# Single PSUM banks in a ring of eight, and score tiles in pairs, in a clustered-attention kernel

## The chip, the cores and the metric

The kernel runs on one core of one Trainium2 chip. The time is the device time of one execution in microseconds, and the number that counts is the median of the runs: 749.23 us over 3 runs (748.53 to 749.55).

## The reference

Three blocks run one after the other. In the first, queries and keys of 16 heads (batch 2, 8 heads, 768 positions, 64 channels) each choose the nearest of 16 centroids, and a query attends only to keys of its own cluster:

```python
q_assign = argmax(q_n . c_n);  k_assign = argmax(k_n . c_n)
mask = q_assign[:, :, :, None] == k_assign[:, :, None, :]
scores = where(mask, scale * q @ k^T, -1e9)
attn = softmax(scores);  x = attn @ v            # (2, 768, 512)

theta = x @ w_theta
y = w_tok_r @ (x * cos(theta)) + w_tok_i @ (x * sin(theta))
u = x + y;  x = u + max(u @ w_ch, 0)

u = x + (x^T @ U @ V)^T
out = u + max(u @ w_ch1, 0) @ w_ch2
```

## The kernel before, in words

Everything is unrolled by hand, and each engine runs its instructions in the order in which the Python code issues them. `manual_schedule` keeps that order. A tile is allocated when the code asks for it, from the tiles of its pool whose last use has been issued; the instruction that first writes it waits until that last use is over.

*Memory.* 59 SBUF slots of 128x768 fp32 serve all large tiles (`slot`, L52). PSUM has eight banks. Six form three tiles of two banks (`ps2`, L55); two more form one tile for the value product and, later, for every second theta and feed-forward tile (`pv2`, L58).

*Attention* goes over 8 clusters of work `g`: two heads of one batch entry. (The word cluster below means such a unit.) The mask is folded into the score product as one-hot rows. Precision comes from splitting fp32 numbers into a high and a low part, so scores take two passes. For each cluster:
- `assign_items` (L101) finds the nearest centroid: one group of matmuls (`sims`), then six VectorE operations. `split_hi`, `split_lo`, `pack` (L173 to L214) split queries and keys on ScalarE and GpSimd and copy the parts into packed tiles by DMA from SP, and `mask_rows` or `mask_direct` write the one-hot rows.
- `max_tile` (L225) multiplies a tile of 128 queries with all keys (two matmuls of 384 columns, into two banks) and VectorE takes the maximum of 768 columns (L233). `max_rows` (L242) turns the maxima into two rows of the packed tile, so that they are subtracted by the score product.
- `scores` (L259) makes one tile of 128 keys by 768 queries with four matmuls of 384 columns, and ScalarE takes the exponential of all 768 (L267).
- `pv` (L270) multiplies by the values; `sum_keys` (L284) sums the exponentials; `row_sums`, `spread`, `norm_x` divide.

In `attention` (L656) the loop over `g` has six steps `p`. A step issues two score tiles of cluster `g` and two maximum tiles of cluster `g+1` in turn (`ORDER`, L659), then two calls of `pv`, then background work for about 1.7 us of VectorE (`fill`, L636): items of a queue, or else conversions of float64 weights (`Convert`, L320: ScalarE L340 and L357, VectorE L344, L348, L352, GpSimd L361). From `g == 2` on, all twelve token-weight tiles are queued for conversion.

*Prologue* (L732): it loads constants, then queries and keys of clusters 0 and 1, the values of cluster 0, and queries and keys of clusters 2 and 3, nine loads of 384 KB in all; prepares the centroids; and carries cluster 0 through assignment, maxima and the first head's scores. `heat` issues matmuls that only keep TensorE running.

*Mixer* (L825): theta and token mixing over 24 steps, channel mixing (`chmix`), the low-rank block (`low1`, `low2`) and the feed-forward block (`ff1`, `ff2`), whose sums go to the output from `ff_sum` (L620).

Of the kernel before, what the change touches and what calls it, by code (L numbers as in the profile page):

```python
# [10 lines left out]
F32 = mybir.dt.float32  # L11
# [11 lines left out]
P = 128  # L23
# [17 lines left out]
def tile_cluster_block(ctx: ExitStack, tc: tile.TileContext, qk, v, cent, wth, wr, wi, wch,  # L41
# [7 lines left out]
    pp = ctx.enter_context(tc.tile_pool(name="pp", bufs=3, space=PSUM))  # L49
    pv_p = ctx.enter_context(tc.tile_pool(name="pvp", bufs=1, space=PSUM))  # L50
# [4 lines left out]
    def ps2(name, shape=None):  # L55
        return pp.tile(shape or [P, 2, 512], F32, tag="ps", name=name)

    def pv2(name):  # L58
        return pv_p.tile([P, 2, 512], F32, tag="pv", name=name)
# [41 lines left out]
    def assign_items(g):  # L101
        st = {}

        def sims():
            ps = ps2("sims")
            for i, hf, o in BLOCKS:
                nc.tensor.matmul(out=ps[o:o + 32, 0, :HALF], lhsT=cblk[:, g % NP, :], rhs=raw[g, i][:, cols(hf)],
                                 start=True, stop=True)
            st["s"] = slot("s_t")[:, :HALF]
            nc.vector.transpose(st["s"], ps[:, 0, :HALF])  # L110
# [42 lines left out]
    def mask_direct(g, h, eng):  # L153
        x = XROW[h]
        r = slice(x, x + 16)
        for i in range(2):
            ps = ps2("oht")
            for hf in range(2):
                o = 32 * (2 * i + hf) + 16 * h
                nc.tensor.matmul(out=ps[r, hf, :HALF], lhsT=identb[:, o:o + 16], rhs=onehots[g],  # L160
                                 start=True, stop=True)
            src, dst = ps[r, :, :HALF], h2((qp, kp)[i][g % SETS, h, 0][r])
            if i == 0:
                nc.scalar.activation(out=dst, in_=src, func=AF.Copy)
            elif eng is nc.scalar:
                nc.scalar.activation(out=dst, in_=src, func=AF.Identity, scale=BIG, bias=kmul[r, 2:3])
            else:
                eng.tensor_scalar(dst, src, BIG, BIG, op0=ALU.mult, op1=ALU.subtract)
# [33 lines left out]
    def pack(g, main=(0, 1)):  # L202
        s = g % SETS
        qh, ql, kh, kl = hl[g, 0, 0], hl[g, 0, 1], hl[g, 1, 0], hl[g, 1, 1]
        for h in range(2):
# [10 lines left out]
    def pack_direct(g, h):  # L216
        d, s = slice(64 * h, 64 * h + 64), g % SETS
        for t, src in ((kp[s, h, 0], raw[g, 1]), (qp[s, h, 0], raw[g, 0]), (qp[s, h, 1], raw[g, 0])):
            nc.scalar.activation(out=t[d], in_=src[d], func=AF.Copy)
        nc.gpsimd.tensor_tensor(kp[s, h, 1][d], raw[g, 1][d], f32(kp[s, h, 0][d]), op=ALU.subtract)  # L220


    mx_t = {}

    def max_tile(g, h, qt):  # L225
        s = g % SETS
        if qt == 0:
            mx_t[g, h] = small.tile([P, NT], F32, tag="mx", name="mx")
        ps = ps2("smax")
        for hf in range(2):  # L230
# [734 lines left out]
```

## Time and profile before

| what | value |
|---|---|
| median of 3 runs | 749.23 us |
| the profiled execution | 750.61 us, its span 748.8 us |
| TensorE busy (matmul) | 711.7 us, 95% |
| VectorE | 436.9 us, 58% |
| ScalarE | 294.4 us, 39% |
| GpSimd | 196.8 us, 26% |
| DMA | 64.03 MB, mean 86 GB/s |
| mean granted clock of TensorE | 0.986 |
| loads of queries and keys | 384 KB each, 16 of them |

The span is the time from the first to the last instruction. Busy times of a TensorE row add matmuls that overlap in its pipeline, so a busy share near 100% does not mean that no matmul came late; its weight loads (PEld) are separate instructions, and where one of them waits, the reason is written behind the row. The clock is a share of full speed.

### The profile page before, as it was taken

To read this page: it belongs to the slowest core of one execution; us is meant where nothing else is said; L and a number is where in the kernel's file an instruction comes from. 1 tells how busy PE (TensorE), PEld (TensorE's weight loads), DVE (VectorE), ACT (ScalarE), POOL (GpSimd) and SP (SyncE) were. 2 spreads that over 40 slices of the span, in tenths; PEclk is the share of its full clock that TensorE was granted. 3 is DMA by queue.
4 is the path that set the end of the run, shared out by engine and by line. 5 is a ranking of instruction groups with operands and counts; after the bars stand their busy time and mean duration, and the time that the engine had idled before them with its cause. 6 is when DMAs were issued, how large, how long until landed. Compare 5 with 4: busy or idle time off the path is not lost.

```text
span 748.8 us, 10420 instructions
## 1 busy us (share of the span) xinstructions
PE 711.7 (95%) x4111; PEld 557.9 (75%) x4111; DVE 436.9 (58%) x658; ACT 294.4 (39%) x485; POOL 196.8 (26%) x191
## 2 busy tenths in 40 slices
PE   6799999999899998999999799999999999999997
PEld 2555555555555558999999799888889888888885
DVE  6775877768778538545759796543543533532222
ACT  4454555545556554454653823322222222211000
POOL 8512032132433316111327450132112112100000
PEclk8799999999999999999999999999999999999999
DMA  8776385563622213000311221012212211000112
GB/s 242 172 184 214 84 215 168 127 177 99 162 71 84 85 55 115 1 1 1 113 43 54 85 84 43 1 43 85 84 43 85 85 47 67 29 1 0 57 34 79
DMA packets 21504, 64.03 MB, mean 86 GB/s; under 512 B 4272, under 2 KB 6192, under 8 KB 21456
## 3 DMA queue, kind: packets, MB, share of 16 engines
q1 hardware_dynamic: 21456, 63.37, 29.5%
q8 instruction: 32, 0.52, 0.3%
q14 instruction: 16, 0.13, 0.1%
HBM read 40.94 MB, written 3.15 MB: 59 GB/s over the span
## 4 chain that ended last, share of the span: by engine, by line
PE 83%; DVE 7%; ACT 4%; DMA 2%; issue 2%; POOL 2%; SPq 0%; DVEq 0%; POOLq 0%; ACTq 0%
PE acc L610 18%; PE g L589 17%; PE y L477 10%; PE pv L274 9%; PE st L264 8%; PE smax L231 5%; PE h L493 5%; PE l L291 4%; PE th L435 3%; DVE mx L233 2%; PE h L544 1%; DVE tht L443 1%; DMA qp<-lo 1%; DVE cv L348 1%; ACT p L267 1%
## 5 line engine op out<-in xcount | busy, mean ns | idle before, releaser
L361 POOL TENSOR_TENSOR wl<-cv,wh 128x768 fp32r<-128x768 f32 (+1 forms) x40 | 78.3, 1958 | 256.6 <-ACT wh L357 228.3
L596 DVE SCALAR_TENSOR_TENSOR gl<-g,gh 128x512 fp32r<-128x512 f32 x48 | 33.2, 692 | 156.6 <-ACT gh L594 156.6
L267 ACT ACTIVATE p<-st 128x768 f32<-128x768 f32 x96 | 76.9, 811 | 89.8 <-PE st L264 87.2
L233 DVE TENSOR_REDUCE mx<-smax 128x1 f32<-128x768 f32 x96 | 90.3, 953 | 35.4 <-PE smax L231 35.0
L594 ACT ACTIVATE gh<-g 128x512 fp32r<-128x512 f32 x48 | 28.7, 598 | 204.2 <-PE g L589 204.2
L477 PE MATMUL y<-wh,z 128*128 128x384 f32 x384 | 89.4, 345 | 8.0 <-ACT z L455 6.8
L264 PE MATMUL st<-qp,kp 128*128 128x384 f32 x384 | 88.8, 356 | 3.9 <-ACT p L267 1.7
L589 PE MATMUL g<-ul,wh 128*128 128x512 f32 (+1 forms) x256 | 86.4, 337 | 0.0
L589 PE MATMUL g<-uh,wh 128*128 128x512 f32 (+1 forms) x256 | 86.1, 336 | 0.0
L589 PE MATMUL g<-uh,wl 128*128 128x512 f32 (+1 forms) x256 | 86.0, 336 | 0.0
L264 PEld LDWEIGHTS st<-qp,kp 128*128 128x128 f32 x384 | 66.6, 192 | 25.1 <-issue 10.2
L610 PE MATMUL acc<-gh,wh 128*128 128x512 f32 x192 | 76.0, 396 | 0.6 <-DVE xT L566 0.6
L610 PE MATMUL acc<-gl,wh 128*128 128x512 f32 x192 | 75.7, 394 | 0.0
L610 PE MATMUL acc<-gh,wl 128*128 128x512 f32 x192 | 75.7, 394 | 0.0
L477 PEld LDWEIGHTS y<-wh,z 128*128 128x128 f32 x384 | 67.5, 190 | 9.3 <-ACT z L455 7.7
L274 PE MATMUL pv<-p,v 128*64 128x384 f32 x384 | 72.4, 501 | 0.0
L231 PE MATMUL smax<-kp,qp 128*128 128x384 f32 x192 | 55.7, 375 | 6.5 <-DVE mx L233 2.8
L589 PEld LDWEIGHTS g<-uh,wh 128*128 128x128 f32 x256 | 48.5, 189 | 6.2
L589 PEld LDWEIGHTS g<-ul,wh 128*128 128x128 f32 x256 | 48.4, 189 | 5.9
L589 PEld LDWEIGHTS g<-uh,wl 128*128 128x128 f32 x256 | 48.6, 190 | 5.2
L274 PEld LDWEIGHTS pv<-p,v 128*64 128x64 f32 x384 | 23.5, 136 | 34.8 <-issue 34.8
L477 PE MATMUL y<-wl,z 128*128 128x384 f32 x192 | 49.4, 339 | 0.0
(127 smaller groups left out, 1183.6 us busy)
## 6 DMA issues: line engine op xcount, KB each, us to landing
st<-in_w_dram SPq DMA_DIRECT2D x20, 768.0 KB, 4.2
raw<-in_qk_dram SPq DMA_DIRECT2D x16, 384.0 KB, 5.7
qp<-hi SPq DMA_DIRECT2D x30, 192.0 KB, 2.8
st<-in_wr_dram SPq DMA_DIRECT2D x6, 768.0 KB, 4.2
st<-in_wi_dram SPq DMA_DIRECT2D x6, 768.0 KB, 4.3
v<-in_v_dram SPq DMA_DIRECT2D x8, 384.0 KB, 4.8
kp<-hi SPq DMA_DIRECT2D x32, 96.0 KB, 2.8
qp<-lo SPq DMA_DIRECT2D x32, 96.0 KB, 2.6
```

The lines of the kernel that those rows point to most:

```text
L231: nc.tensor.matmul(out=ps[:, hf, :HALF], lhsT=qp[s, h, 0][:, qt * P:(qt + 1) * P], rhs=kp[s, h, 0][:, hf * HALF:(hf + 1) * HALF], start=Tr ...
L233: nc.vector.tensor_reduce(mx_t[g, h][:, qt:qt + 1], ps[:, :, :HALF], axis=AX.XY, op=ALU.max)
L264: nc.tensor.matmul(out=ps[:, hf, :HALF], lhsT=kp[s, h, w][:, kt * P:(kt + 1) * P], rhs=qp[s, h, w][:, hf * HALF:(hf + 1) * HALF], start=(w ...
L267: nc.scalar.activation(out=h2(t), in_=ps[:, :, :HALF], func=AF.Exp, scale=float(D) ** -0.5)
L274: nc.tensor.matmul(out=pvt[g][64 * h:64 * h + 64, hf, :HALF], lhsT=v_t[g][:, kt, 64 * h:64 * h + 64], rhs=pt[g, h, kt][:, hf * HALF:(hf + ...
L291: nc.tensor.matmul(out=ps[o:o + 32, 0, :HALF], lhsT=ones, rhs=pt[g, h, kt][:, cols(hf)], start=(kt == 3 * a), stop=(kt == 3 * a + 2))
L361: nc.gpsimd.tensor_tensor(t[:, :c.w], c.t, f32(c.hi[:, :c.w]), op=ALU.subtract)
L477: nc.tensor.matmul(out=yps[u, j][:, hf, :HALF], lhsT=lhs, rhs=w[st][e][:, hf * HALF:(hf + 1) * HALF], start=(st == 0 and n == 0), stop=(st ...
L493: nc.tensor.matmul(out=ps[:, hf, :HALF], lhsT=wv[a], rhs=xs[b, t][c][:, hf * HALF:(hf + 1) * HALF], start=(n == 0), stop=(n == 11))
L589: nc.tensor.matmul(out=ps[:, o:o + w], lhsT=wv[a], rhs=us[b, t][e][:, s0:s0 + w], start=(n == 0), stop=(n == 11))
L596: nc.vector.scalar_tensor_tensor(gl, ps, 0.0, f32(gh), op0=ALU.max, op1=ALU.subtract)
L610: nc.tensor.matmul(out=aps[c, e // 2][:, e % 2], lhsT=wv[a], rhs=g[x], start=(first and i == 0), stop=(last and i == 2))
```

## The change

Every PSUM tile becomes one bank of a ring of eight (`bank`); what needs two takes two tiles (`banks`), and its reader becomes two instructions, one per bank. Score tiles and maximum tiles are made in pairs of tiles, 1536 columns in three banks of 512: the first tile's columns 0 to 511; its last 256 beside the next tile's first 256; and the rest. ScalarE's exponentials go by the pieces (512, 256, 256, 512 columns); VectorE takes maxima of each bank, and a join takes the larger of each two.

The order of attention is by pairs too, so the value products of a cluster begin later and the last of them come in step 3 of the next; normalisation moves from step 3 to step 5. Six of the twelve token-weight tiles are queued only in the last cluster, where `fill` gets twice the budget. In the prologue, loads of clusters 2 and 3 and of the values come later, the second low split and the direct low part (`pack_direct_lo`, split off `pack_direct`, L216) come after the masks on GpSimd, the packs of cluster 0 are issued head by head, and the second cluster's assignment runs while cluster 0's maxima are turned into rows.

```diff
-    pp = ctx.enter_context(tc.tile_pool(name="pp", bufs=3, space=PSUM))
-    pv_p = ctx.enter_context(tc.tile_pool(name="pvp", bufs=1, space=PSUM))
+    pp = ctx.enter_context(tc.tile_pool(name="pp", bufs=8, space=PSUM))
+    def bank(name):
+        return pp.tile([P, 512], F32, tag="ps", name=name)
+    def banks(name):
+        return [bank(name), bank(name)]
...
+    THIRDS = [[(0, 0, 512)], [(0, 512, 256), (1, 0, 256)], [(1, 256, 512)]]
+    def max_pair(g, h, a):
+        s = g % SETS
+        if a == 0:
+            mx_t[g, h] = small.tile([P, 2 * NT], F32, tag="mx12", name="mx12")
+        o = 2 * a
+        for part in THIRDS:
+            ps, c = bank("smax"), 0
+            for j, k0, w in part:
+                nc.tensor.matmul(out=ps[:, c:c + w], lhsT=qp[s, h, 0][:, (a + j) * P:(a + j + 1) * P],
+                                 rhs=kp[s, h, 0][:, k0:k0 + w], start=True, stop=True)
+                c += w
+            n = len(part)
+            nc.vector.tensor_reduce(mx_t[g, h][:, o:o + n], ps.rearrange("p (n w) -> p n w", n=n), axis=AX.X, op=ALU.max)
+            o += n
...
+    def scores_pair(g, h, a):
+        s = g % SETS
+        for kt in (a, a + 1):
+            pt[g, h, kt] = slot(f"p{h}")
+        for part in THIRDS:
+            ps, c = bank("st"), 0
+            for j, q0, n in part:
+                for w in range(2):
+                    nc.tensor.matmul(out=ps[:, c:c + n], lhsT=kp[s, h, w][:, (a + j) * P:(a + j + 1) * P],
+                                     rhs=qp[s, h, w][:, q0:q0 + n], start=(w == 0), stop=(w == 1))
+                c += n
+            c = 0
+            for j, q0, n in part:
+                nc.scalar.activation(out=pt[g, h, a + j][:, q0:q0 + n], in_=ps[:, c:c + n], func=AF.Exp,
+                                     scale=float(D) ** -0.5)
+                c += n
...
     def ff2(c, f):
...
+            if last:
                 ff_sum(c, e, end)
...
-        ORDER = [(0, 0), (0, 1), (0, 2), (0, 3), (0, 4), (1, 0), (0, 5), (1, 1), (1, 2), (1, 3), (1, 4), (1, 5)]
+        ORDER = [(0, 0), (0, 2), (0, 4), (1, 0), (1, 2), (1, 4)]
...
+                conv_load.extend(tok[:6])
+                late = tok[6:]
+            if g == 7:
+                conv_load.extend(late)
...
+                if order[p]:
+                    h, a = order[p]
+                    scores_pair(g, h, a)
+                    if h:
+                        pvq.extend((g, kt, hf) for kt in (a, a + 1) for hf in range(2))
+                if nxt:
+                    max_pair(g + 1, p // 3, 2 * p % 6)
+                    if p % 3 == 2:
+                        max_join(g + 1, p // 3)
...
-                fill(1.7)
+                fill(1.7 if nxt else 3.4)
...
+        its, its1 = assign_items(0), assign_items(1)
         for i in range(2):
             split_hi(0, i)
-            split_lo(0, i, nc.gpsimd)
+        split_lo(0, 0, nc.gpsimd)
         run(its[:1])
         pack_direct(0, 0)
+        pack(0, main=(), heads=(0,))
+        load_v(0)
+        for i in range(2):
+            load_raw(2, i)
+
         init_packs(1, nc.gpsimd)
         heat(14)
         run(its[1:])
+        run(its1[:1])
         mask_direct(0, 0, nc.vector)
+        split_lo(0, 1, nc.gpsimd)
+        pack_direct_lo(0, 0)
+        pack(0, heads=(1,))
         for i in range(2):
             split_hi(1, i)
+        for a in (0, 2, 4):
+            max_pair(0, 0, a)
+        max_join(0, 0, act=True)
+        max_rows(0, 0)
+
+        run(its1[1:])
+        mask_direct(0, 1, nc.scalar)
+        init_packs(2, nc.gpsimd)
+        for i in range(2):
             split_lo(1, i, nc.gpsimd)
         pack(1)
+        for g in range(3, 4):
+            for i in range(2):
+                load_raw(g, i)
         bg.extend(split_items(2, nc.gpsimd))
+        for a in (0, 2, 4):
+            scores_pair(0, 0, a)
+            max_pair(0, 1, a)
+            heat(2)
+            if a == 2:
+                mask_direct(1, 0, nc.scalar)
                 while bg:
                     fill(.5)
+        max_join(0, 1)
         max_rows(0, 1)
         mask_direct(1, 1, nc.scalar)
```

## Rows read from the trace of the kernel before

**Rows 1.** The page, busy time, share and instructions of each engine.
```profile
PE 711.7 (95%) x4111; PEld 557.9 (75%) x4111; DVE 436.9 (58%) x658; ACT 294.4 (39%) x485; POOL 196.8 (26%) x191
```

**Rows 2.** Stretches: length, busy us and count by engine, clock, DMA share, GB/s.
```profile
0.00:41.60 41.60, 29.67 (x123) 16.07 (x124) 27.11 (x51) 20.28 (x28) 29.50 (x35) 0.84 0.81 207
...
62.80:245.80 183.00, 173.63 (x1106) 102.11 (x1104) 137.59 (x196) 100.54 (x129) 53.91 (x71) 0.99 0.52 140
245.80:274.50 28.70, 28.70 (x200) 15.03 (x198) 12.12 (x16) 16.70 (x22) 8.62 (x11) 1.00 0.26 83
274.50:291.00 16.50, 13.32 (x94) 12.41 (x90) 13.47 (x22) 9.03 (x21) 7.37 (x12) 1.00 0.33 102
```

**Rows 3.** Waits of weight loads in clusters 1 to 6: us, times, longest.
```profile
PEld smax L231 <- ACT p L267: 8.2, 27, 2.3
...
PEld smax L231 <- DVE mx L233: 4.1, 6, 0.7
```

**Rows 4.** Timeline of one attention step, TensorE: start us, us, instruction [idle before].
```profile
107.49 0.96 PE L264 MATMUL st<-qp,kp 128*128 128x384 f32 x4
...
109.42 0.30 PEld L231 LDWEIGHTS smax<-kp,qp 128*128 128x128 f32 x2 [0.24 <-ACT p L267]
...
109.97 1.51 PE L274 MATMUL pv<-p,v 128*64 128x384 f32 x8
...
111.41 0.31 PEld L247 LDWEIGHTS <-m 128*2 128x2 bf16 x6 [0.60 <-DVE mx L233]
```

**Rows 5.** The page, costliest groups: busy us, mean ns | idle before.
```profile
L596 DVE SCALAR_TENSOR_TENSOR gl<-g,gh 128x512 fp32r<-128x512 f32 x48 | 33.2, 692 | 156.6 <-ACT gh L594 156.6
...
L233 DVE TENSOR_REDUCE mx<-smax 128x1 f32<-128x768 f32 x96 | 90.3, 953 | 35.4 <-PE smax L231 35.0
L594 ACT ACTIVATE gh<-g 128x512 fp32r<-128x512 f32 x48 | 28.7, 598 | 204.2 <-PE g L589 204.2
```

**Rows 6.** Groups by line and shape, 45 to 270 us, ScalarE's exponentials.
```profile
L267 ACT ACTIVATE p<-st 128x768 f32<-128x768 f32 x89 | 71.3, 811 | 85.4 <-PE st L264 82.9 <-DMA qp<-hi 1.1 <-DMA raw<-in_qk_dram 0.3
```

**Rows 7.** The chain that ended last: start us, us, what.
```profile
8.48 9.51 DMA qp<-lo
22.21 3.56 DVE mx L233 x4
...
88.59 2.14 PE l L291 x24
...
295.39 4.17 PE y L477 x24
...
487.55 2.76 PE g L589 x12
...
493.11 2.87 PE g L589 x24
```

**Rows 8.** Timeline of the prologue, 0 to 45 us.
```profile
6.54 3.58 POOL L180 TENSOR_TENSOR lo<-raw,hi 128x768 fp32r<-128x768 f32 x2
...
8.24 4.06 DVE L118 TENSOR_TENSOR eqw<-s_t,mxc 128x384 bf16<-128x384 f32 x1
...
10.09 1.79 POOL L220 TENSOR_TENSOR kp<-raw,kp 64x768 fp32r<-64x768 f32 x1
...
15.79 0.96 DVE L168 TENSOR_SCALAR kp<-oht 16x768 fp32r<-16x768 f32 x1 [1.30 <-PE oht L160]
...
18.13 1.62 PE L231 MATMUL smax<-kp,qp 128*128 128x384 f32 x4 [0.64 <-DMA qp<-lo]
...
27.73 0.80 ACT L249 ACTIVATE qp<-mrow 2x768 fp32r<-2x768 f32 x1 [4.09 <-PE mrow L247]
```

**Rows 9.** Waits of matmuls over the whole span: us, times, longest.
```profile
PE h L493 <- DVE xT L497: 1.1, 2, 0.8
...
PE acc L610 <- DVE xT L566: 0.6, 1, 0.6
```

**Rows 10.** Timeline of the end: VectorE's last two adds.
```profile
744.29 1.40 DVE L625 TENSOR_TENSOR xT<-acc,xT 128x512 f32<-128x512 f32 x2 [0.35 <-PE acc L610]
```

More of the change, by code (lines that the diff above doesn't have):

```diff
@@ L244, in max_rows @@
         m2 = mx_t.pop((g, h))
-        ps = ps2("mrow")
-        for qt in range(NT):
-            nc.tensor.matmul(out=ps[x:x + 2, qt // 3, (qt % 3) * P:(qt % 3 + 1) * P], lhsT=m2[:, qt, :],
-                             rhs=identb, start=True, stop=True)
-        nc.scalar.activation(out=h2(qp[s, h, 1][x:x + 2]), in_=ps[x:x + 2, :, :HALF], func=AF.Copy)
+        for hf in range(2):
+            ps = bank("mrow")
+            for j in range(3):
+                nc.tensor.matmul(out=ps[x:x + 2, j * P:(j + 1) * P], lhsT=m2[:, 3 * hf + j, :], rhs=identb,
+                                 start=True, stop=True)
+            nc.scalar.activation(out=qp[s, h, 1][x:x + 2, cols(hf)], in_=ps[x:x + 2, :HALF], func=AF.Copy)
     pt, v_t, pvt, xT = {}, {}, {}, {}
@@ L482, in ymix @@
                 x = xT[2 * u + j]
-                nc.vector.tensor_tensor(h2(x), yps[u, j][:, :, :HALF], h2(x), op=ALU.add)
+                for hf in range(2):
+                    nc.vector.tensor_tensor(x[:, cols(hf)], yps[u, j][hf][:, :HALF], x[:, cols(hf)], op=ALU.add)
     def chmix(b, e):
-        ps = ps2("h")
+        ps = banks("h")
         n = 0
@@ L496, in chmix @@
         x = xT[b * NP + e]
[L497 removed]
+        for hf in range(2):
+            nc.vector.scalar_tensor_tensor(x[:, cols(hf)], ps[hf][:, :HALF], 0.0, x[:, cols(hf)], op0=ALU.max, op1=ALU.add)
     xt4 = {}
@@ L601, in ff2 @@
         if first:
-            for j in range(2):
-                aps[c, j] = ps2("acc")
+            for e in range(4):
+                aps[c, e] = bank("acc")
         g = gt.pop((c, f))
         end = last and f == NF - 1
-        order = (0, 2, 1, 3) if end and c == 2 else (0, 1, 2, 3)
-        for e in order:
+        for e in range(4):
             wv = wcol(w2_t, f * DM + e * P, P)
             for i, (a, x) in enumerate(PASSES):
-                nc.tensor.matmul(out=aps[c, e // 2][:, e % 2], lhsT=wv[a], rhs=g[x],
+                nc.tensor.matmul(out=aps[c, e], lhsT=wv[a], rhs=g[x],
                                  start=(first and i == 0), stop=(last and i == 2))
-            if end and c == 2 and e:
-                ff_sum(c, {2: 0, 1: 2, 3: 1}[e], end)
-            elif last and e % 2 and not (end and c == 2):
-                ff_sum(c, e - 1, end)
+            if last:
                 ff_sum(c, e, end)
-        if end and c == 2:
-            ff_sum(c, 3, end)
     def ff_sum(c, e, end):
@@ L734, in prologue @@
         nc.vector.memset(hot[:, :512], 0.0)
-        hp = pv2("hot")
+        hp = bank("hot")
         def heat(n):
             for _ in range(n):
-                nc.tensor.matmul(out=hp[:, 0], lhsT=hot[:, :P], rhs=hot[:, :512], start=True, stop=True)
+                nc.tensor.matmul(out=hp, lhsT=hot[:, :P], rhs=hot[:, :512], start=True, stop=True)
         nc.sync.dma_start(out=cst_sb, in_=cst)
```

165 lines of the change are left out of this document (57 added, 108 removed).

## The prediction

> **What bounds the kernel now.** TensorE is busy 711.7 of 748.8 us [rows 1], so I first read the table of stretches, which says where it is not, and then what it waits for there. Four stretches matter [rows 2]: the prologue (to 41.6, TensorE busy 29.67, granted clock 0.84), clusters 1 to 6 of attention (183.0 us, 173.63 busy), cluster 7 (28.7, no gap) and the start of the mixer (16.5, 13.32 busy). In the rest of the mixer the chain of waits is matmul behind matmul, so little can come from there.
>
> "Busy" hides stalls, since matmuls overlap, so for the clusters I read the weight loads, which stop at once when a bank is missing: those of the maxima waited 8.2 us for the exponentials of the tile before and 4.1 us for VectorE's maxima [rows 3]. That is a ring of three two-bank tiles at work: the second maxima of a step take the pair that the step's first exponential still reads. The timeline of one step shows the size [rows 4]: it runs from 107.49 to 111.41, 3.92 us, of which 0.24 are this wait; after it the first value product starts 0.55 us behind the last maxima's first weight load, though their two matmuls are worth 0.35.
>
> **The change part by part.** Prices first. ScalarE takes 0.598 us for 512 columns [rows 5] and 0.811 for 768 [rows 6]: 0.83 ns a column and 0.17 fixed, so I estimate 0.49 for 384 and 0.385 for 256. VectorE takes 0.953 for 768 and 0.692 for 512 [rows 5], about 0.17 fixed too. Matmuls cost 4.17/24 = 0.174 us at 384 columns, 2.76/12 = 0.230 at 512, 2.87/24 = 0.120 at 256 [rows 7].
>
> *Score and maximum pairs.* The eight score matmuls of a step become four of 512 and four of 256: 1.40 for 1.39 us; the maxima's four cost 0.70 both before and after. So the new widths cost TensorE nothing. A step is then 1.40 + 0.70, 0.2 for the last matmul's run into the value products, and 1.44 for these (109.97 to 111.41): 3.74 us. A cluster adds two key sums of 2.14 [rows 7] and, estimated from their columns, 1.4 for the rows of maxima and the assignment matmuls: 28.1 against 183.0/6 = 30.5. Six clusters could give 14 us; the two waits of [rows 3] alone are 12.3. With eight banks, two held by the value product, a bank comes back after six others, one whole step later. Against it: ScalarE gets four exponentials for two, 1.97 us for 1.62 a pair, and VectorE three maxima for two, 2.08 for 1.91, with two short joins a cluster. VectorE goes from 137.59/6 = 22.9 us a cluster to about 24.4, ScalarE from 16.8 to about 19.4; both stay under 28.1 [rows 2], and that slack is the cover. If it goes, nothing is gained here. The range is 3 to 14; I take 10.5, nearest the waits named, with some left because VectorE would be 87% busy.
>
> *Halved copies* (value output, maxima rows, sums in the mixer): 0.17 us more each on ScalarE or VectorE, hidden by TensorE's work. The deferred value products and the later normalisation add no work.
>
> *Weights held back to cluster 7.* Six of the twelve token-weight tiles now come there, with twice the filling. VectorE has room: 12.12 busy of 28.7 [rows 2]; so has GpSimd. ScalarE does not: 16.7 us now, plus the splits and up to six conversions, makes about 26, and an exponential queued behind a conversion holds the value products that need it. I take 1 us slower, between 0 and 3. The loads are issued from SP, whose queue holds no other load by then, and need a staging buffer free, not ScalarE. In return the mixer starts without conversions between the short VectorE operations of theta: of its 3.2 us of idle TensorE [rows 2] I take 2 back, between 0 and 3.2.
>
> *Prologue.* VectorE's comparison in the first assignment took 4.06 us [rows 8], because it ended only 0.42 after GpSimd's third subtraction (10.09 + 1.79 = 11.88). The change leaves one 1.79 us subtraction in front (6.54 to 8.33), so the comparison ends near 8.75, 3.55 earlier. The mask was written 4.45 us after it (16.75 against 12.30); with the second cluster's transpose put ahead, 13.8. The maxima were then held until 18.13 by a pack copy issued at 8.48 that took 9.51 us to land [rows 7, 8]; of the nine bulk loads of 384 KB ahead of it the change leaves four, so I let it land before 13.8. Nine maxima of 0.69 take 6.2, the join and its rows 2.6 (before: 25.77 to 28.53): 22.9 against 28.5. Then ScalarE sets the pace: two masks of four copies at 0.49, twelve exponentials of three pairs (5.9), two splits of 0.8: 11.4, and I add 0.7 for matmuls between them at the mean clock of 0.84 [rows 2]. Attention starts at 35 against 41.6. The second cluster's assignment, 3.5 us of VectorE, lies under masks and scores. GpSimd's list (one subtraction, eight memsets, two subtractions, eight memsets, two subtractions) ends near 28, and SP issues the sixteen copies of cluster 1 behind it, the first landing near 30: in time. Loads of clusters 2 and 3 come later on SP, cluster 3's behind all of these, but are used only in attention. The gain is 6.5, between 4 (comparison alone) and 9 (TensorE at full clock throughout, and no pause between ScalarE's pieces).
>
> *Mixer and tail.* The waits of channel-mix matmuls (1.1) and of the first accumulator (0.6) for VectorE [rows 9] go with eight banks. At the end two adds stood behind the last matmul (1.40 for two) [rows 10]; now one does: 0.7. Together 2.3, between 1.4 and 2.9.
>
> The sum is -10.5 + 1 - 2 - 6.5 - 2.3 = -20.3 us. The profiled execution took 750.61 (span 748.8), 1.4 above the median of 749.23, so it would become 730.3 and the median 728.9; I say 729.
>
> **The rivals.** *The fixed costs reach the path.* VectorE and ScalarE run in order, and TensorE may follow them after all: clusters then give nothing and the splits are paid. For it: VectorE was already 75% busy with waits of its own. Against: its waits for key sums shrink, and a bank is now due a step later. Without the 10.5 the time is 739.4, and to 741 with some of the fixed cost. The Trainium skill (VectorE: DVE Perf Modes, section on the TRN2 errata) says that each instruction of VectorE or ScalarE pays a fixed latency again, and advises tiles of 512 elements or more; by it the 256- and 384-wide pieces are a mistake, and 96 more exponentials by the 0.17 above would put 16 us onto the path, for 745 at worst. The rows agree on the fixed cost but show ScalarE at 100.54 of 183.0 us. Chance 0.17.
>
> *The prologue's gain is hidden.* The scores of cluster 0 or the packs of cluster 1 arrive late, since GpSimd's memsets now stand before the second low split: 749.2 - 13.8 = 735.4. The landing of small copies under load (9.51 us) speaks for it, GpSimd's list above against it. Chance 0.11.
>
> *Slower: SBUF slots.* Value products lag by two calls more and both probability tiles of a pair are taken at once, from the same 59 slots. A slot freed less than a step ago makes ScalarE's first exponential of a pair wait, behind it all other ScalarE work, and then the banks. In the trace an exponential waited once, 1.1 us, for a copy still reading its slot [rows 6]. At 1.1 us for each of 36 pairs it costs 39.6: 768. It decides from 20.3/36 = 0.56 us a pair. Against: it happened once in 89, and weight tiles and splits that held slots move to cluster 7. Chance 0.06.
>
> *The ring is none:* were the bank freed last handed out first, each third would wait for its reader, and a step would take about double. The rows speak against it: the second scores of a step start right behind the first maxima. Chance 0.01.
>
> **How the numbers follow.** The forecast has 0.65, with 723 to 735 as its own range. The range reaches to the fixed-cost case and down to the sum of the better ends: 721 to 741. A measurement of this kernel tells about 0.2%, 1.5 us, from no change. Faster 0.92, same 0.02, slower 0.06.
>
> **What would show it.** Right: weight loads of the maxima no longer wait for exponentials or maxima; clusters 1 to 6 take 28.5 to 29 us each; first attention maxima near 35 us, first maxima near 14; six weight conversions in cluster 7; one add after the last matmul. Wrong: VectorE without idle time in the clusters, ScalarE waiting for slots or for copies, or TensorE idle in cluster 7 behind exponentials.

## The result, and the profile after

The changed kernel takes 736.27 us (median of three runs, 735.71 to 737.27) against 749.39 for the kernel before in the same comparison: 13.1 us less, a ratio of 0.983 (95% interval 0.981 to 0.985). One more run of it was disturbed and took 1751.66 us; it is left out here, as are two such runs of r1_halves below, and with it the median is 736.77, the 736.8 that the expectations below name. The profiled execution took 736.27 us, its span is 734.5, that is 14.3 less than the profiled span of before.

First the table of stretches again, cut where the stages now begin (length, busy us and count of TensorE, its weight loads, VectorE, ScalarE, GpSimd, then clock, DMA share, GB/s):

```profile
0.00:40.86 40.86, 28.96 (x123) 15.65 (x123) 26.88 (x59) 22.35 (x43) 29.81 (x35) 0.85 0.78 199
40.86:60.36 19.50, 19.50 (x120) 10.86 (x119) 16.01 (x32) 7.50 (x18) 0.00 (x0) 0.97 0.69 178
60.36:232.36 172.00, 167.11 (x1107) 95.56 (x1105) 136.83 (x241) 100.07 (x215) 51.97 (x69) 0.99 0.56 150
232.36:267.64 35.28, 31.46 (x208) 14.46 (x206) 25.89 (x25) 23.25 (x45) 18.66 (x15) 1.00 0.35 112
```

Against [rows 2] the prologue hardly moved (40.86 for 41.60), clusters 1 to 6 lost 11.0 us (172.0 for 183.0), cluster 7 gained 6.6 (35.28 for 28.70), and what follows, the mixer to the end, went from 474.3 to 466.9. Cluster 0 lost 1.7, of which 1.44 are two calls of the value product that the change moves to the end, into cluster 7. The time lies inside the range, 7.3 above the forecast, and two of the terms are far off.

**Where the gain is.** The waits of the weight loads in clusters 1 to 6 (total, times, longest), to be set beside [rows 3]:

```profile
PEld smax L237 <- DVE mx L241: 2.2, 2, 1.2
...
PEld l L318 <- ACT p L292: 2.0, 1, 2.0
```

The maxima no longer wait for an exponential at all (8.2 us before), and for VectorE in two places only. The timeline shows what a step is now, on TensorE, VectorE and ScalarE, answering to [rows 4]:

```profile
96.12 1.68 PE L287 MATMUL st<-qp,kp 128*128 128x512 f32 x8
97.64 0.85 PE L237 MATMUL smax<-kp,qp 128*128 128x512 f32 x4
98.42 1.51 PE L300 MATMUL pv<-p,v 128*64 128x384 f32 x8
99.86 1.69 PE L287 MATMUL st<-qp,kp 128*128 128x512 f32 x8
...
98.06 1.89 DVE L241 TENSOR_REDUCE mx<-smax 128x1 f32<-128x512 f32 x3 [0.79 <-PE smax L237]
...
100.64 1.64 ACT L292 ACTIVATE p<-st 128x512 f32<-128x512 f32 x4 [2.10 <-PE st L287]
```

From 96.12 to 99.86 it is 3.74 us, the figure of the forecast. The last two lines show why the thinner pieces cost nothing: four exponentials in a row take 1.64 us, not the 1.97 of the working, and three maxima 1.89 instead of 2.08.

The gain is not even. Clusters 1 to 6 took 29.3, 29.5, 30.3, 29.5, 33.6 and 30.8 us before and take 25.1, 29.4, 28.1, 28.5, 29.9 and 31.1 after: clusters 1 and 5 alone give 7.9 of the 11.0. Cluster 5 of before holds a stretch at the lower clock behind a wait of 2.3 us for exponentials (the longest of [rows 3]):

```profile
181.47:215.05 33.58, 30.83 (x190) 17.96 (x188) 24.04 (x36) 17.80 (x23) 11.09 (x13) 0.95 0.42 100
```

After has such a stretch too, in cluster 6 (granted clock 0.95, last section), so the two nearly cancel in the sum. What still keeps cluster 5 of after over 28.1 is a slot: ScalarE's exponentials stand for 2.66 us, though their scores are there, until VectorE's comparison (L118) has read the slot that they write; TensorE's key sum stands behind them:

```profile
179.66 0.87 ACT L292 ACTIVATE p<-st 128x512 f32<-128x512 f32 x2 [2.66 <-DVE eqw L118]
180.31 2.14 PE L318 MATMUL l<-p,ones 128*32 128x384 f32 x24 [1.71 <-ACT p L292]
```

In the built program the first of these exponential tiles has the slot in which the comparison's input lay. In cluster 2 the key sum waits 1.25 us for VectorE's maxima.

**Where it was lost: cluster 7.** The chain of waits holds two entries that it did not have (start, us, what), two loads of weights that are still to be converted:

```profile
242.19 4.22 DMA st<-in_wr_dram
...
257.15 4.17 DMA st<-in_wi_dram
```

The timeline of cluster 7 shows who stands behind them:

```profile
241.22 0.89 DVE L379 SCALAR_TENSOR_TENSOR cv<-st,cv 128x768 int32<-128x768 int32 x1
...
246.49 0.91 ACT L367 ACTIVATE cv<-st 128x768 f32<-128x768 f32 x1 [6.46 <-DMA st<-in_wr_dram]
247.29 1.61 ACT L292 ACTIVATE p<-st 128x512 f32<-128x512 f32 x4
...
247.93 1.76 PE L287 MATMUL st<-qp,kp 128*128 128x512 f32 x8 [0.81 <-ACT p L292]
251.69 1.51 PE L300 MATMUL pv<-p,v 128*64 128x384 f32 x8 [2.00 <-ACT p L292]
...
261.40 0.91 ACT L367 ACTIVATE cv<-st 128x768 f32<-128x768 f32 x1 [3.39 <-DMA st<-in_wi_dram]
```

VectorE's low bits (L379) free a staging buffer at 242.1, the load issues at 242.19 and lands 4.2 us later. Meanwhile ScalarE, which works in order, is already at that tile's first operation, the magnitude (L367), and stands idle for 6.46 us; the exponentials stand behind it, TensorE behind them. Without any wait cluster 7 would take the 28.7 us of before and the 1.44 of the moved value products, 30.1: some 5.1 us are lost here.

**Where it was won and lost again: the prologue.** Timeline of all engines, to be read with [rows 8]:

```profile
8.42 0.56 DVE L118 TENSOR_TENSOR eqw<-s_t,mxc 128x384 bf16<-128x384 f32 x1
...
13.27 2.35 PE L237 MATMUL smax<-kp,qp 128*128 128x512 f32 x12 [1.24 <-ACT qp L163]
...
20.53 0.86 ACT L268 ACTIVATE qp<-mrow 2x384 fp32r<-2x384 f32 x2 [0.84 <-PE mrow L266]
...
20.98 1.85 DVE L124 TENSOR_TENSOR eqw<-eqw,cvals 128x384 bf16<-128x384 bf16 x1
...
27.85 0.49 PE L237 MATMUL smax<-kp,qp 128*128 128x512 f32 x1
29.12 0.50 PE L237 MATMUL smax<-kp,qp 128*128 128x256 f32 x2 [0.78 <-DVE mx L241]
30.41 0.49 PE L237 MATMUL smax<-kp,qp 128*128 128x512 f32 x1 [0.79 <-DVE mx L241]
...
31.69 1.21 PE L160 MATMUL oht<-eqw,identb 128*16 128x384 bf16 x4 [0.33 <-DVE mx L241]
...
40.86 1.56 PE L237 MATMUL smax<-kp,qp 128*128 128x512 f32 x4
```

Up to the rows of the first head's maxima (written at 21.39, before at 28.53) the new order wins 7.1 us, a little more than forecast. Then it loses 6.4. Between 27.85 and 31.69 TensorE and VectorE take turns: each maxima matmul starts when the reduction just before it has ended. That is what one bank looks like, and in the built program the three maxima tiles of this pair and the first mask tile indeed got the same bank, since the pool does not hand banks out in turn. The same happens once more, to one pair of cluster 6; the other 46 pairs have three banks each.

### The profile page after: what moved, and what is told of

Its sections match the earlier page's. It is cut to its first block, busy times and chain, and to the rows that moved or that the text cites. A ratio compares the mean times of both kernels' runs of the same rounds, so it can differ in the third digit from the quotient of the medians.

```text
span 734.5 us, 10599 instructions
## 1 busy us (share of the span) xinstructions
PE 704.6 (96%) x4110; PEld 551.4 (75%) x4110; DVE 441.1 (60%) x746; ACT 299.4 (41%) x613; POOL 198.3 (27%) x191
## 3 DMA queue, kind: packets, MB, share of 16 engines
q1 hardware_dynamic: 21456, 63.37, 30.2%
## 4 chain that ended last, share of the span: by engine, by line
PE 84%; DVE 9%; ACT 4%; DMA 2%; issue 1%; POOL 0%; SPq 0%; DVEq 0%; ACTq 0%; POOLq 0%
PE g L617 18%; PE acc L637 18%; PE y L503 10%; PE st L287 9%; PE pv L300 8%; PE h L520 5%; PE smax L237 4%; PE l L318 4%; PE th L461 4%; DVE mx L241 2%; PE h L572 1%; DVE cv L379 1%; DVE tht L469 1%; DVE cv L375 1%; PE mrow L266 1%
## 5 line engine op out<-in xcount | busy, mean ns | idle before, releaser
L388 POOL TENSOR_TENSOR wl<-cv,wh 128x768 fp32r<-128x768 f32 (+1 forms) x40 | 81.6, 2042 | 224.3 <-ACT wh L384 197.7
L624 DVE SCALAR_TENSOR_TENSOR gl<-g,gh 128x512 fp32r<-128x512 f32 x48 | 33.2, 692 | 155.7 <-ACT gh L622 155.7
L622 ACT ACTIVATE gh<-g 128x512 fp32r<-128x512 f32 x48 | 28.7, 598 | 202.0 <-PE g L617 202.0
L241 DVE TENSOR_REDUCE mx<-smax 128x1 f32<-128x512 f32 x144 | 90.4, 682 | 29.7 <-PE smax L237 29.7
L292 ACT ACTIVATE p<-st 128x512 f32<-128x512 f32 x192 | 78.9, 495 | 70.4 <-PE st L287 59.6
L287 PE MATMUL st<-qp,kp 128*128 128x256 f32 (+1 forms) x384 | 83.4, 360 | 1.0 <-ACT p L292 0.8
L287 PEld LDWEIGHTS st<-qp,kp 128*128 128x128 f32 x384 | 56.8, 194 | 28.1 <-issue 12.6
L379 DVE SCALAR_TENSOR_TENSOR cv<-st,cv 128x768 int32<-128x768 int32 (+2 forms) x42 | 47.7, 1137 | 0.9
```

Of the source, the lines that this page charges most:

```text
L241: nc.vector.tensor_reduce(mx_t[g, h][:, o:o + n], ps.rearrange("p (n w) -> p n w", n=n), axis=AX.X, op=ALU.max)
L287: nc.tensor.matmul(out=ps[:, c:c + n], lhsT=kp[s, h, w][:, (a + j) * P:(a + j + 1) * P], rhs=qp[s, h, w][:, q0:q0 + n], start=(w == 0), st ...
L292: nc.scalar.activation(out=pt[g, h, a + j][:, q0:q0 + n], in_=ps[:, c:c + n], func=AF.Exp, scale=float(D) ** -0.5)
L379: nc.vector.scalar_tensor_tensor(t, self.lw, 29, t, op0=ALU.logical_shift_right, op1=ALU.bitwise_or)
L388: nc.gpsimd.tensor_tensor(t[:, :c.w], c.t, f32(c.hi[:, :c.w]), op=ALU.subtract)
L624: nc.vector.scalar_tensor_tensor(gl, ps, 0.0, f32(gh), op0=ALU.max, op1=ALU.subtract)
```

## Experiments

The twelve kernels change only the order of the work, its banks or (r1_halves) the widths of its pieces. Their stages, each from one profiled execution, in us; each ratio is to the kernel before in the same comparison, whose medians lie between 748.4 and 749.4:

| run | attention starts | clusters 1 to 6 | cluster 7 | mixer to end | median of runs | ratio to before (95%) |
|---|---|---|---|---|---|---|
| before | 41.6 | 183.0 | 28.7 | 474.3 | 749.39 | |
| after | 40.9 | 172.0 | 35.3 | 466.9 | 736.27 | 0.983 (0.981 to 0.985) |
| c1_early | 41.6 | 170.4 | 32.0 | 466.1 | 732.02 | 0.978 (0.975 to 0.981) |
| c2_lag | 40.1 | 172.1 | 30.1 | 468.7 | 733.94 | 0.980 (0.978 to 0.982) |
| c1_fill17 | 43.2 | 172.1 | 30.0 | 473.5 | 739.10 | 0.986 (0.982 to 0.989) |
| r1_halves | 35.4 | 180.6 | 35.4 | 466.1 | 743.47 | 0.994 (0.991 to 0.997) |
| p3_oldpro | 37.7 | 176.3 | 35.3 | 466.0 | 737.71 | 0.985 (0.983 to 0.988) |
| p1_order | 37.9 | 170.4 | 35.3 | 466.8 | 734.28 | 0.981 (0.978 to 0.984) |
| p2_zero_later | 40.8 | 172.1 | 35.3 | 468.8 | 738.20 | 0.986 (0.982 to 0.990) |
| ring6 | 36.9 | 173.3 | 36.5 | 471.3 | 744.06 | 0.993 (0.991 to 0.996) |
| m1_early_lag | 40.1 | 168.6 | 30.2 | 472.0 | 731.46 | 0.979 (0.975 to 0.983) |
| f1_early_p1 | 38.6 | 170.4 | 31.7 | 466.5 | 729.28 | 0.974 (0.973 to 0.976) |
| f2_all_repairs | 40.7 | 170.6 | 31.2 | 465.4 | 729.84 | 0.976 (0.973 to 0.980) |
| f3_no_first_wait | 40.9 | 167.4 | 31.2 | 466.4 | 724.01 | 0.967 (0.965 to 0.969) |

Equal code differs between executions. With the new order of the prologue the first maxima started between 13.1 and 15.2, and attention between 40.1 and 43.2 in the five kernels whose whole prologue is that of after (after, c1_early, c2_lag, c1_fill17, m1_early_lag); so effects in the prologue are better read from the first head's rows on, where these five take 20.0 to 21.3 us. The mixer of p2_zero_later, which is that of after, took 1.9 longer. Cluster 6 of equal code takes 31.1 or 29.5, by the clock (last section). And a profiled execution can lie some us off the median of its kernel: ring6 and r1_halves 3.7 and 3.1 below, f3_no_first_wait 4.0 above.

### Cluster 7: does ScalarE wait, or is it full?

```diff
-                conv_load.extend(tok[:6])
-                late = tok[6:]
-            if g == 7:
-                conv_load.extend(late)
+                conv_load.extend(tok)
```

> All twelve token-weight tiles are queued at cluster 2 again, none is held back to cluster 7; everything else is the changed kernel (736.8 us). Theory: cluster 7 is 5.1 us too long because ScalarE, which runs in order, stands at a conversion whose staging load has not landed, and the exponentials stand behind it. Then cluster 7 (35.25 us) falls to about 30, clusters 2 to 6 keep 28.7 to 29.3 each, and the time is 732 to 735. Rival: VectorE and ScalarE are full, the conversions cost the same wherever they lie; clusters 2 to 6 grow by what cluster 7 loses and the time is 736 to 738.

Measured: cluster 7 31.95, none of clusters 1 to 6 longer, 732.0 us. The theory holds; the rival, by which the other clusters would grow, falls. What is left over 30 holds one more such wait of ScalarE, 3.51 us at 248.38. Of the 4.1 us by which this span is shorter, 1.6 are cluster 6 at the full clock.

```diff
-                    if conv_in:
+                    if conv_in and not lag[0]:
                         conv_in[0].magnitude()
```

(`lag` is set from cluster 7's start to the end of attention; the magnitude is then a filling step of its own.)

> The six tiles stay in cluster 7; only the first ScalarE operation of each conversion (the magnitude) is issued one filling step later instead of right behind the low bits of the tile before, so that the staging load has had time and fewer exponentials stand behind it. Theory (ScalarE waits for staging loads, 6.46 and 3.39 us in two places): these two waits shrink below 2 us, cluster 7 goes from 35.25 to 31 to 33, the time to 733 to 735. Rival (ScalarE has simply too much work in cluster 7, busy 26 of 35 us): the waits go and cluster 7 stays over 34, the time within 1 us of 736.8.

Measured: cluster 7 30.12, better than expected, 733.9 us. Of the two waits of ScalarE 0.95 us are left of the 3.39, and of the 6.46 this:

```profile
245.53 0.93 ACT L367 ACTIVATE cv<-st 128x768 f32<-128x768 f32 x1 [2.42 <-DMA st<-in_wr_dram]
```

These waits fell by 6.5 us and cluster 7 by 5.2. But a part of the work left it too: ScalarE is busy 21.9 us there for 23.3 and VectorE 16.7 for 25.9, and the mixer grew by 1.8. That ScalarE was not full but waited is shown more cleanly by f3_no_first_wait below: there it waits for no load in cluster 7, VectorE is busy 23.2 us, and the cluster takes 31.2.

### What relieves the mixer: holding back, or the doubled filling?

```diff
-                fill(1.7 if nxt else 3.4)
+                fill(1.7)
```

(on top of c1_early)

> All twelve tiles queued at cluster 2 (as in the run all early, 732.0 us) and cluster 7 filled at the single rate again, so that the conversions which do not fit in go on in the mixer. Theory: what relieves the start of the mixer is the doubled filling of cluster 7, not the holding back: cluster 7 gets 1 to 2 us shorter than 31.95 and the mixer 1.5 to 4 us longer than 466.05, the time is 732 to 735. Rival: the conversions in the mixer are hidden there, cluster 7 gains and the mixer stays within 0.7 us: 729.5 to 731.5.

Measured: cluster 7 30.03 and the mixer 473.5, 7.4 longer than in c1_early; 739.1 us. The direction is the theory's, the size twice what it expected. The waits of weight loads in the mixer, of c1_fill17:

```profile
PEld y L503 <- ACT z L481: 7.7, 3, 5.1
PEld y L503 <- POOL z L487: 3.4, 1, 3.4
```

and of c1_early, whose only such wait this is:

```profile
PEld y L503 <- ACT z L481: 5.1, 2, 4.5
```

So the doubled filling, not the holding back, takes conversions off the mixer: for 1.9 us in cluster 7 it gives back up to 7.4. Holding back alone (after against c1_early) gives the mixer nothing (466.9 and 466.1). Not all of the 7.4 are the waits (11.1 against 5.1): between 262 and 300 the granted clock is 0.91 in c1_fill17 and 1.00 in c1_early, by an estimate from that share 3.4 us. How the two overlap was not taken apart; the four runs of c1_fill17 lie between 734.8 and 740.2.

### Clusters 1 to 6: is it the number of banks, or thirds?

```diff
-    THIRDS = [[(0, 0, 512)], [(0, 512, 256), (1, 0, 256)], [(1, 256, 512)]]
+    THIRDS = [[(0, 0, 384)], [(0, 384, 384)], [(1, 0, 384)], [(1, 384, 384)]]
```

(the reduction reads the columns used)

> Two tiles of scores or maxima lie in four banks of 384 columns instead of three of 512; eight banks as before. ScalarE's four exponentials and VectorE's maxima cost about the same (4 x 0.49 for 1.97 us, 4 x 0.53 for 2.08). A step then takes 8 banks of the 6 that the value product leaves, not 6. Theory (what counts is that a bank comes back only after a whole step): weight loads of maxima and scores wait again, steps are 3.85 to 4.0 us for 3.74, clusters 1 to 6 take 29.5 to 30.5 each for 28.7, the time is 741 to 746. Rival (single banks instead of two-bank tiles are what counts, thirds add nothing): 736 to 738, no more waits of TensorE than now.

Measured: 30.1 us a cluster for 28.7, 743.5 us (eight runs from 739.5 to 748.8); the theory holds, single banks alone are not enough. The waits are back, for VectorE's maxima above all:

```profile
PEld smax L237 <- DVE mx L241: 8.4, 13, 1.8
...
PEld smax L237 <- ACT p L292: 2.3, 2, 2.0
```

One reservation: two of the six clusters (33.2 and 32.7 us) hold a stretch at the lower clock level behind such a wait (granted clock 0.95 in each), after has one. By an estimate from these shares the clock makes 3.3 us here and 1.6 in after, so some 1.7 of the 8.6 us are not the waits themselves. The same run starts attention at 35.4: with halves two pairs of the prologue's second head have one bank twice, but as their first and their fourth, and no maxima go by turns.

### The prologue: order, GpSimd, or banks?

The old order (loads, splits, packs, assignment) with the new banks and pairs; the diff is that of the change's prologue, backwards, with `max_pair` and `scores_pair` for the single tiles.

> The prologue's order of the kernel before (loads, splits, packs, assignment of the second cluster after the first maxima) with the single banks and pairs of the changed kernel; attention and mixer are those of the changed kernel. Theory: the new order won 7 us up to the first head's rows of maxima and lost them again after, so by itself it is worth little: attention starts at 40 to 43 us for 40.85 and the time is 736 to 739. Rival: the old order would suffer from the single banks, and the new one is worth the forecast 6 us: attention starts at 45 or later, the time is over 740.

Measured: attention starts at 37.7, 3.2 us earlier than with the new order; 737.7 us. The total is the theory's, but not its reason. No pair has a bank twice in this prologue, so it compares with the new order where none does either: 36.9 in ring6 and 37.9 in p1_order. The early start is lost in cluster 6 (34.6 us for 31.1), where VectorE came late to one pair in one bank:

```profile
PEld smax L237 <- DVE mx L241: 4.4, 2, 3.4
```

after which TensorE ran at the lower clock level for some 6 us (granted clock 0.90 in cluster 6).

```diff
-        run(its1[1:])
         mask_direct(0, 1, nc.scalar)
...
             max_pair(0, 1, a)
             heat(2)
+            if a == 0:
+                run(its1[1:])
```

> In the prologue VectorE takes the second cluster's assignment after the second head's first pair of maxima, not before it. Theory (the assignment stands ahead of the maxima on VectorE, which start at 25.95 us though their matmuls start at 24.23): attention starts 1 to 2.5 us earlier, at 38.4 to 39.9, and the time is 734 to 736. Rival (ScalarE's masks, splits and exponentials set this part, as the forecast had it): attention starts at 40 to 42 and the time is 736 to 738.

Measured: attention starts at 37.85, 734.3 us; the theory's time, and the pace is not ScalarE's. (Cluster 6 at the full clock has 1.6 us of this execution's gain.) The three maxima that went by turns are now one group on TensorE:

```profile
26.64 0.85 PE L237 MATMUL smax<-kp,qp 128*128 128x512 f32 x4
...
37.85 1.47 PE L237 MATMUL smax<-kp,qp 128*128 128x512 f32 x4
```

Here two things moved at once, since with VectorE's order the handing out of the banks changed too and no pair of the prologue has a bank twice. The next two runs part them.

```diff
-        init_packs(2, nc.gpsimd)
         for i in range(2):
             split_lo(1, i, nc.gpsimd)
         pack(1)
+        init_packs(2, nc.gpsimd)
```

> In the prologue GpSimd's eight memsets of the third pack set come after the two subtractions of cluster 1 instead of before them. Theory (two of VectorE's assignment operations took 1.85 and 1.95 us for 0.36 and 0.56 because GpSimd worked beside them): other GpSimd work now lies beside them; if memsets were the cause, 20.98 falls to 0.36 only where no memset runs, and attention starts 1 to 2.5 us earlier, time 734.5 to 736. Rival (any GpSimd work stretches them, or the subtractions do it more): they stay at 1.8 us or more and the time is 736 to 739.

Measured: attention starts at 40.8, 738.2 us: the rival's time, though 1.9 of it are the longer mixer. VectorE's two operations did shrink, beside the memsets, and the maxima still go by turns in one bank:

```profile
22.45 0.36 DVE L124 TENSOR_TENSOR eqw<-eqw,cvals 128x384 bf16<-128x384 bf16 x1
...
30.13 0.51 PE L237 MATMUL smax<-kp,qp 128*128 128x256 f32 x2 [0.79 <-DVE mx L241]
```

So 3 us less on VectorE did not end the turns. Attention starts no earlier because the first maxima started 1.5 us later than in after; from the first head's rows on it takes 19.4 us, 0.6 to 2.0 less than the five kernels with the prologue of after.

```diff
-        return pp.tile([P, 512], F32, tag="ps", name=name)
+        lo, n = TURN.get(name, (0, 6) if name in ATT else (0, 8))
+        k = seat.get((lo, n), 0)
+        seat[lo, n] = (k + 1) % n
+        return pp.tile([P, 512], F32, tag=f"ps{lo + k}", name=name)
```

(each tag one bank; `TURN` gives hot and pv banks 6 and 7, y and g 0 to 3, th and acc 4 to 7)

> The changed kernel with its banks handed out in strict turn: six go round among scores, maxima, masks, sums and rows of maxima, two are kept for the value products (and the warm-up matmuls), in the mixer four for y or g and four for theta or acc. Nothing else differs. Theory: the pool as it is gives one and the same bank to the three maxima of one pair where it takes the other banks for still occupied, once in the prologue (there to a mask tile too) and once in cluster 6, and TensorE and VectorE then work by turns. In strict turn attention starts at 38 to 39.7 us for 40.86, cluster 6 takes 28.5 to 30 us for 31.1, the other clusters stay, and the time is 732 to 735. Rival: those maxima are late because VectorE is late; strict turn then changes nothing or makes a step wait for the slowest exponential: 736 to 740.

Measured: attention starts at 36.9 and cluster 6 takes 27.4, both better than the theory expected, with nothing but the banks changed; yet the time is 744.1, worse than both said. From the first head's rows (their first matmul) to attention it takes 17.1 us, the five kernels with the prologue of after 20.0 to 21.3: one bank for one pair costs some 3 us here. (With p1_order's order it is 17.7 to 18.4, in f2 and f3 below too, whose attention starts late only because their first maxima did, at 15.0 and 15.2.) The loss lies elsewhere, and the profiled execution, at 740.3, shows a part of it: the mixer is 4.4 longer (weight loads of g wait 4.6 us there, 0.4 in after), cluster 7 is 1.2 longer at a granted clock of 0.95, and cluster 2 takes 33.6 for 29.4, also at 0.95, with this on ScalarE and TensorE:

```profile
109.99 0.90 ACT L374 ACTIVATE cv<-st 128x768 f32<-128x768 f32 x1 [4.38 <-DMA st<-in_wr_dram]
...
111.42 3.84 PE L325 MATMUL l<-p,ones 128*32 128x384 f32 x24 [3.74 <-ACT p L299]
```

It is the wait of cluster 7 again, in a cluster with filling at the single rate; in after it is there too (4.28 us), but the key sum did not wait for the exponentials behind it. That a step waits for exponentials is what the rival had said of strict turn.

### The repairs together

Both conversion repairs, `lag` set for the whole of attention:

> Both repairs of the conversions at once: all twelve tiles queued at cluster 2, and in the whole of attention the magnitude is issued a filling step later. Theory (the two waits of ScalarE add up): cluster 7 falls from 31.95 us (all early) to about 30, clusters 1 to 6 stay, the time is 729.5 to 731.5. Rival (what the later step leaves over is paid in the mixer, which grew by 1.8 us in the run with the later magnitude alone): 731.5 to 734.

Measured: clusters 2 to 5 take 28.08 us each, alike to 0.01 and equal to the 28.1 that the forecast worked out for a cluster without waits; cluster 7 30.2. But the mixer grows by 5.1 over after, because a step of its own for each magnitude leaves conversions over (57 of ScalarE's conversion operations lie in the mixer, 53 in after): 731.5, and the rival is right in that.

c1_early and p1_order together:

> Two repairs together: all twelve tiles queued at cluster 2, and in the prologue the second cluster's assignment behind the second head's first pair of maxima. Theory: they act in different stages, so the gains add: attention starts near 37.9, cluster 7 takes 32, the mixer 466, the time is 727.5 to 729.5. Rival: what both runs won in cluster 6 (29.5 us for 31.1 in each) is won once only and the rest is partly lost to other clock dips: 729.5 to 731.5.

Measured: 729.3 us, 7.0 under after, where the two alone gave 4.3 and 2.0. The rival's share, cluster 6 at 29.5, is in each of the three profiled executions and can count only once, so how exactly the gains add stays open; both effects are there (attention at 38.6, cluster 7 at 31.7).

```diff
+                if conv_in and conv_in[0].t is None:
+                    conv_in[0].magnitude()
                 if p == 3 and g + 2 < NG:
```

(on top of f1: behind each pair's maxima, at no step; the filling stops at a conversion whose magnitude is not issued; the GpSimd splits of clusters 6 and 7 come at their fourth and fifth pair)

> The two repairs of the run before, and: the magnitude of a conversion is issued only behind the next pair's scores and maxima, at no filling step of its own; the splits of the mixer's first inputs on GpSimd come in the middle of clusters 6 and 7 instead of at their start. No three maxima of a pair share a bank any more. Theory: clusters 2 to 5 fall to 28.1 each (as with both conversion repairs), cluster 6 to 28 to 29.5, cluster 7 to 30 to 31, and the mixer stays at 466 to 467 since no conversions are left over: 722 to 726. Rival: conversions are again left over and the mixer pays 2 to 5 us for them: 726 to 730.

Measured: 729.8 us (728.9 to 734.6), the rival's range, for a reason that neither had named: the mixer stayed at 465.4, but cluster 1 took 28.3 for 25.1, as ScalarE met the very first load just issued (below). Clusters 2 to 5 took 28.5, 28.1, 28.1 and 29.2, not 28.1 each: in cluster 5 TensorE still waits 1.05 us for exponentials, with no load that ScalarE waits for.

```profile
66.60 0.89 ACT L367 ACTIVATE cv<-st 128x768 f32<-128x768 f32 x1 [4.25 <-DMA st<-in_wth_dram]
```

```diff
-                if conv_in and conv_in[0].t is None:
+                if g + p > 1 and conv_in and conv_in[0].t is None:
```

> The kernel of all repairs (729.8 us) with one condition more: the first magnitude of all is not issued in the first pair of cluster 1, where its staging load has just been issued. Theory: in cluster 1 ScalarE stood 4.25 us at that magnitude, for the same reason as in cluster 7 of the changed kernel, and the rows of maxima and exponentials behind it held TensorE (28.29 us for 25.1 in every other run). Then cluster 1 falls to 25.1 to 25.5, the other stages stay, the time is 725.5 to 727.5. Rival: the conversion that starts one pair later is missing at the end and the mixer pays: 728 to 730.

Measured: cluster 1 25.11, 724.0 us, 12.3 under the changed kernel and 24.4 under the one before (748.38 in this comparison): the version that beats both. The median is better than the theory said. The profiled execution is the slowest of its five (728.0) and 0.9 us under f2's; of its stages only cluster 1 got clearly shorter.

## Why the prediction was right in sign and range, and wrong in two of its terms

The forecast was 729 within 721 to 741, and 736.3 came. By spans the terms were these.

- **Score and maximum pairs, -10.5: came as -11.0.** The mechanism is the one named (the ring of three), shown by the waits that went and by r1_halves, which brings most of the time back. That the size came so close is in part luck: 7.9 of it lie in clusters 1 and 5, and the sum holds a stretch at the lower clock on either side. Nor do the single clusters keep to the forecast's 28.5 to 29; only their mean does. Two sizes in the working were off and did no harm: VectorE was put at 24.4 us a cluster and ScalarE at 19.4, and they take 136.83/6 = 22.8 and 100.07/6 = 16.7, for an instruction in a row costs less than one alone (three maxima 1.89 us, one alone 0.69). With that the rival of the fixed costs falls: four thinner pieces in a row do not pay the fixed part four times. The Trainium skill's rule that went into that rival (VectorE: DVE Perf Modes, section on the TRN2 errata: a fixed latency for each instruction, so tiles of 512 and more) would have had ScalarE longer; the row of 1.64 us for four against 0.811 each for two [rows 6] does not show it. The section gives its advice for operations that read SBUF, and the exponentials and maxima here read PSUM. What was still missing to 28.1 is the slot of cluster 5 (1.71 us), VectorE's late maxima in cluster 2 (1.25) and the clock in cluster 6. In m1_early_lag, where conversions fall elsewhere, the first two waits are gone; that ScalarE's staging loads were their cause is not shown, since f3_no_first_wait has none of these left and cluster 5 still takes 29.2.
- **Weights held back to cluster 7, +1: came as +6.6, of which 1.44 are the moved value products.** The step that failed is the sentence that the loads "need a staging buffer free, not ScalarE". It is true and looks the wrong way: the load does not need ScalarE, but ScalarE needs the load, 4.2 us after VectorE's low bits, with the exponentials behind it in order. TensorE idle in cluster 7 behind exponentials was among the forecast's own signs of being wrong, and it came: 31.46 us busy of 35.28. The forecast did say that an exponential behind a conversion holds the value products; it priced the conversion's work and not its wait.
- **Mixer start, -2, and channel mix and accumulator, -1.7: the mixer gave -7.4.** The waits for VectorE went as said ([rows 9] have no counterpart after); channel mixing gave 1.4 and what follows it 1.7. Token mixing gave 4.4. In its first 16.5 us TensorE is busy 15.32 us for 13.32, the 2 of the forecast; the other 2.4 come later, where the forecast did not look. The forecast credited them to the tiles held back and the doubled filling together; by c1_fill17 it is the filling, for without it token mixing ends 6.6 us later than in after, part of that by the clock.
- **Tail, -0.7: came as 0.** From the start of the last matmul to the end it is 4.24 us before and 4.28 after. [rows 10] were misread: the two adds of 1.40 us start at 744.29, when the last matmul had not begun, so only one of them ever stood behind it. After, four adds run as one group, and again one stands behind the last matmul:

```profile
728.59 2.76 DVE L647 TENSOR_TENSOR xT<-acc,xT 128x512 f32<-128x512 f32 x4 [4.87 <-PE acc L637]
...
730.22 0.40 PE L637 MATMUL acc<-gh,wl 128*128 128x512 f32 x1
```

- **Prologue, -6.5: came as -0.75.** The first half was right to the parts: comparison ended at 8.98 (8.75 forecast), first maxima at 13.3 (near 14), rows written at 21.4 (22.9). The step that failed is "then ScalarE sets the pace", which added up ScalarE's work to 12.1 us and took its cover for granted. It took 19.5, with ScalarE idle between pieces: it waits for TensorE, that for a bank, that for VectorE. Shown are some 3 us for the repeated bank (ring6 alone; p1_order with nearly the same) and, less surely, 0.6 to 2.0 for VectorE's stretched operations (p2_zero_later). The rest of the 7.4 us between 12.1 and 19.5 stays open. That r1_halves starts attention at 35.4, the forecast's 35, is luck: its rows are written at 20.7 for 22.9, and it then takes 14.7 us for 12.1. And in p3_oldpro the old order with the new banks and pairs starts attention at 37.7, 3.9 us earlier than the kernel before and within a us of the new order without a repeated bank (36.9 and 37.9): the reordering, to which the forecast gave the whole 6.5, shows no gain there. What the thirds lose there to the halves even without a repeat was not taken apart.

The rival "the ring is none" had a grain of truth at chance 0.01: the pool does for a ring except at two of 48 pairs, where it is a ring of one. The slots case came twice, in cluster 5, and not in each of 36 pairs: exponentials stood 2.66 us for the slot told above and 3.39 us for one that value products were reading, and TensorE lost 1.7 us. Of the exponentials' 70.4 us of idle time 59.6 ended with their scores, and with the same slots m1_early_lag reaches 28.08 a cluster.

In sum, the prologue came 5.7 us worse than said and cluster 7 5.6 worse, the mixer 3.1 better, cluster 0 1.7 and the six clusters 0.5 better: -20.3 became -14.3 by span. The range held it, but its upper part had been set by the case of the fixed costs, which is not what happened: misses of 11.3 us one way were met by 5.3 the other way, and that the sum stayed inside is luck as much as working.

## What to carry to other kernels

When work is moved onto an engine that runs in order, price its waits, not only its busy time: ask for each moved operation what it needs, when that is issued, and what stands behind it. A pool of single banks is a ring only as far as the banks are really handed out in turn; look for matmuls that start just when the reduction before them ends. Before costing "the last instruction of a group", compare its start with the end of what it is said to wait for.

## What was not expected of the hardware

A short wait of TensorE can cost more than itself. In cluster 6 the same one-bank pair is met by after and by p1_order, and the waits of the weight loads are equal (1.22 and 0.99 us in both); in after the key sum behind them ran at the lower clock level (1.2 GHz), 3.52 us for 2.14, in p1_order it did not. The stretch of cluster 6, of after:

```profile
201.24:232.36 31.12, 29.55 (x183) 16.20 (x181) 20.31 (x35) 15.92 (x35) 10.47 (x12) 0.95 0.16 52
```

and of p1_order:

```profile
199.07:228.56 29.49, 27.92 (x182) 15.82 (x180) 20.29 (x35) 15.93 (x35) 10.50 (x12) 1.00 0.16 55
```

The 1.6 us between them are clock alone (TensorE's busy time has them, 29.55 for 27.92), which is why equal code can differ by so much here.

VectorE's low bits, an operation with two inputs in SBUF, took 2.19 us beside GpSimd's subtractions for the usual 0.95, just there, ahead of that pair's maxima. The timeline of VectorE and GpSimd in after:

```profile
204.97 2.19 DVE L379 SCALAR_TENSOR_TENSOR cv<-st,cv 128x768 int32<-128x768 int32 x1
...
204.51 4.33 POOL L448 TENSOR_TENSOR xl<-xT,xh 128x768 fp32r<-128x768 f32 x2 [5.84 <-ACT xh L446]
```

The Trainium skill (SBUF — State Buffer, section "Who interferes with whom") has a rule for this: a VectorE instruction with two inputs in SBUF contends with a GpSimd instruction that reads SBUF. The rows agree. It exempts GpSimd's memsets; p2_zero_later agrees with that too (0.36 us at 22.45 beside memsets), but the 1.85 us at 20.98 in after lie beside memsets as well, and what stretched that one operation stays open.
